# A normalizer sum moved from the tensor engine to the vector engine, and the normalizer used three MLP tiles later

## Chip, cores, metric

The kernel runs on one core of a Trainium2 chip. The metric is the device time of one execution in microseconds (us), lower is better. PE is the tensor engine, PEld its weight loads, DVE the vector engine, ACT the scalar engine, POOL the GpSimd engine, SP the engine that issues most DMAs (40 of 64 issues in the trace of the kernel before). A trace covers one execution from its first to its last recorded instruction (the span); the timed figure is some 2 us longer than the span.

## The reference, cut to what matters

```python
x = A_x                                        # [1, 2048, 512], bf16
phi = lambda t: where(t > 0, t + 1, exp(t)) + 1e-6
pq, pk = phi(q), phi(k)                        # 32 heads of 16
kv  = einsum("bhsd,bhse->bhde", pk, v)
z   = einsum("bhsd->bhd", pk)                  # <- the sum in question: over all 2048 tokens
num = einsum("bhqd,bhde->bhqe", pq, kv)
den = einsum("bhqd,bhd->bhq", pq, z)[..., None] + 1e-6
a   = merge_heads(num / den) @ wo
b   = token_mlp(layernorm(x))                  # w1: 2048 -> 1792, gelu, w2: 1792 -> 2048
g   = sigmoid((x * gate_w).sum(-1, keepdims=True))
out = g * a + (1 - g) * b
```

## The kernel before: the parts that matter

Tokens are cut into 16 tiles of 128. The order on PE is: *key steps* (kacc = x Wk for a tile, then gacc += x^T pk with a lag of four tiles), *query steps* (three uacc matmuls of the MLP and four qacc matmuls per step), *MLP tiles* (sixteen uacc matmuls each, numbered 3 to 13), and *output tiles* (four aps and fourteen yps matmuls each).

The sum z is taken over tokens. Tokens lie in 16 tiles x 128 partitions, so there are two sums: over the tiles and over the partitions. Before, both were matmuls. The first one takes the sixteen pk tiles through a 128x32 selector in four column tiles of the array (the sixteen take 1.24 us in the chain below; sixteen full ones would take 16 x 0.216 = 3.46):

```python
def z_tile(t):
    g = t % 4
    mm(zacc[32 * g : 32 * g + 32, :], zsel[:], pk[:, t, :], t < 4, t >= NT - 4,
       tile_position=(0, 32 * g))
...
for t in range(NT - LAG, NT):       # the last four key tiles
    g_tile(t)
    if t == NT - 3:                 # between gacc of tile 13 and of tile 14
        for u in range(NT):
            z_tile(u)
...                                 # DVE: zhi = bf16(zacc); zhl = odd * zhi - zacc
def kv_matmuls():                   # in query step 4
    ...
    zps = bank("zps")
    for j in range(ND):             # the sum over partitions: 4 matmuls of 8 columns
        mm(zps[:, 8 * j : 8 * j + 8], zhl[:, j * P : (j + 1) * P], neg8[:], True, True)
    ...                             # DVE: Z32 = zps * mask
...
for j in range(NB0, NF):            # MLP tiles 3..13
    ...                             # 16 uacc matmuls, gelu on ACT
    if j == NB0:
        den_matmuls()               # 16 column-tiled denps matmuls; DVE: rden = 1 / denps
        rden_chain()                # rden to DRAM, 16 broadcast loads rex, 16 pqT *= rex on DVE
    elif j <= NB0 + ND:
        w2_matmul(j - NB0 - 1)
```

The gate sums (sixteen DVE instructions, sum of x times gate_w) stood between the query steps and the reciprocal.

Of the kernel before, what the change touches and what calls it, by code (L numbers as in the profile page):

```python
# [8 lines left out]
ALU = mybir.AluOpType  # L9
AX = mybir.AxisListType  # L10
BF16 = mybir.dt.bfloat16
FP32 = mybir.dt.float32
# [3 lines left out]
def kernel(  # L16
# [13 lines left out]
    nc = tc.nc  # L30
    P = nc.NUM_PARTITIONS
    EPS = 1e-5
    PHI_EPS = 1e-6
    HEAD = 16
# [3 lines left out]
    S, D = X.shape  # L38
    F = B_w1.shape[1]
    NT = S // P  # L40
    ND = D // P
    NF = F // P
    SC = 512
    NSC = S // SC
# [14 lines left out]
    work = ctx.enter_context(tc.tile_pool(name="work", bufs=3))  # L59
    opool = ctx.enter_context(tc.tile_pool(name="opool", bufs=4))  # L60
    dpool = ctx.enter_context(tc.tile_pool(name="dpool", bufs=1, space=bass.MemoryType.DRAM))
    ps = ctx.enter_context(tc.tile_pool(name="ps", bufs=8, space=bass.MemoryType.PSUM))

    def keep(shape, dtype, name):
        return persist.tile(shape, dtype, name=name, tag=name)

    def bank(name, dtype=FP32):
        return ps.tile([P, SC], dtype, name=name, tag="bank")

    xs = keep([P, NT, D], BF16, "xs")  # L70
# [6 lines left out]
    pqT = keep([P, ND, S], BF16, "pqT")  # L77
    pk = keep([P, NT, D], BF16, "pk")
# [2 lines left out]
    W2sb = keep([P, ND, D], BF16, "W2sb")  # L81
    Z32 = keep([P, ND * 40], BF16, "Z32")
    zhi = keep([P, D], BF16, "zhi")
    zhl = keep([P, D], BF16, "zhl")
    odd = keep([P, 1], FP32, "odd")
    neg8 = keep([P, 8], BF16, "neg8")
    zsel = keep([P, 32], BF16, "zsel")
    rden = keep([P, SC], BF16, "rden")
    ident = keep([P, P], BF16, "ident")
    mask = keep([P, P], BF16, "mask")  # L90
    maskH = keep([P, 8], BF16, "maskH")
    gw_b = keep([P, D], BF16, "gw_b")
# [6 lines left out]
    gpre = keep([P, NT], FP32, "gpre")  # L99
# [8 lines left out]
    def mm(o, lhsT, rhs, start, stop, **kw):  # L108
        nc.tensor.matmul(o, lhsT=lhsT, rhs=rhs, start=start, stop=stop, **kw)  # L109
# [39 lines left out]
    for c, (j0, nb) in enumerate(w1_chunks):  # L149
        w = wpool.tile([P, NT, FB * P], BF16, name="w1c", tag="wc")  # L150
        w1c.append(w)
        for t0 in range(0, NT, 8) if c == 0 else (0,):
            t1 = t0 + 8 if c == 0 else NT
            nc.sync.dma_start(
                out=w[:, t0:t1, : nb * P], in_=w1_view[:, t0:t1, j0 * P : (j0 + nb) * P]
# [5 lines left out]
    nc.vector.memset(ones_f[:], 1.0)  # L161
    nc.vector.memset(mhalf[:], -0.5)
    nc.vector.memset(Z32[:], 0.0)
    nc.vector.memset(zsel[:], 0.0)
    nc.vector.memset(zsel[:, 0:2], 1.0)
    nc.vector.memset(neg8[:], -1.0)
    nc.gpsimd.memset(ident[:], 0.0)
    nc.gpsimd.affine_select(
        out=ident[:], in_=ident[:], compare_op=ALU.not_equal, fill=1.0, base=0,
        pattern=[[-1, P]], channel_multiplier=1,  # L170
    )
    nc.vector.tensor_reduce(out=odd[:], in_=ident[:, 1:P:32], op=ALU.add, axis=AX.X)
    block_mask(mask[:].rearrange("p (a b) -> p a b", b=HEAD), P // HEAD, HEAD)
    block_mask(maskH[:].rearrange("p (a b) -> p a b", b=1), 8, 1)

# [64 lines left out]
    def ln_shift(g):  # L240
        s = slice(g * TPC, (g + 1) * TPC)
        nc.vector.scalar_tensor_tensor(  # L242
            out=nmr[:, s], in0=mv[:, s, 0], scalar=-1.0, in1=rstd[:, s],
            op0=ALU.mult, op1=ALU.mult,
        )
# [22 lines left out]
            )  # L268
        phi(pqT[:, j, c * SC : (c + 1) * SC], qacc)

    def z_tile(t):
        g = t % 4
        mm(
            zacc[32 * g : 32 * g + 32, :], zsel[:], pk[:, t, :], t < 4, t >= NT - 4,
            tile_position=(0, 32 * g),
        )

    def ln_step(u):
        ln_stats(u)
        if u % TPC == TPC - 1:  # L280
            ln_rstd(u // TPC)
# [19 lines left out]
    for t in range(HEADS, NT):  # L301
# [8 lines left out]
            ln_apply(t - APPLY)  # L310
        if t % TPC == 0 and t >= 2 * TPC:
            ln_shift(t // TPC - 2)
    zacc = bank("zacc")
    for t in range(NT - LAG, NT):
        g_tile(t)
        if t == NT - 3:
            for u in range(NT):
                z_tile(u)
    ln_shift(2)
    ln_apply(NT - APPLY)  # L320
    nc.vector.tensor_copy(out=zhi[:], in_=zacc[:])
    nc.vector.scalar_tensor_tensor(
        out=zhl[:], in0=zhi[:], scalar=odd[:], in1=zacc[:], op0=ALU.mult, op1=ALU.subtract
    )

    gT = persist.tile([P, ND, D], BF16, name="gT", tag="wk_sb")
    for k in range(ND):
# [5 lines left out]
    def gelu(j, acc):  # L333
        nc.scalar.activation(  # L334
            out=uT[:, j, :], in_=acc[:], func=ACT.Gelu_apprx_tanh, bias=bcol[:, j : j + 1]
        )
# [6 lines left out]
    def kv_matmuls():  # L343
        kvps = bank("kvps")
        for j in range(ND):
            for k in range(ND):
                mm(
                    kvps[:, j * P : (j + 1) * P], wv_sb[:, k, j * P : (j + 1) * P],
                    gT[:, k, j * P : (j + 1) * P], k == 0, k == ND - 1,
                )  # L350
        nc.vector.tensor_tensor(
            out=kvbdT[:], in0=kvps[:].rearrange("p (j d) -> p j d", j=ND),
            in1=mask[:].unsqueeze(1).to_broadcast([P, ND, P]), op=ALU.mult,
        )
        zps = bank("zps")
        for j in range(ND):
            mm(zps[:, 8 * j : 8 * j + 8], zhl[:, j * P : (j + 1) * P], neg8[:], True, True)
        nc.vector.tensor_tensor(
            out=Z32[:].rearrange("p (j m) -> p j m", m=40)[:, :, 0:8],
            in0=zps[:, 0:32].rearrange("p (j m) -> p j m", m=8),  # L360
            in1=maskH[:].unsqueeze(1).to_broadcast([P, ND, 8]), op=ALU.mult,
        )

    def w2_matmul(j):
        wps2 = bank("wps2")
        mm(wps2[:], kvbdT[:, j, :], wo_sb[:, j, :], True, True)
        nc.scalar.activation(out=W2sb[:, j, :], in_=wps2[:], func=ACT.Copy)
# [12 lines left out]
    NB0 = 3  # L380
    accs = [bank("uacc") for _ in range(NB0)]
    for t in range(NT):
        for jj in range(NB0):
            mm(accs[jj][:], w1c[0][:, t, jj * P : (jj + 1) * P], hs[:, t, :], t == 0, t == NT - 1)
        q_block(t)
        if 2 <= t < 2 + LN_LAG:
            ln_step(NT - LN_LAG + t - 2)
        if t == 3 + LN_LAG:
            ln_shift(3)
        if 1 <= t < 5 or 7 <= t < 11:  # L390
            ln_apply(t + 7 if t < 5 else t + 5)
        if t == 1:
            biases()
        if t == 4:
            kv_matmuls()
    for jj in range(NB0):
        gelu(jj, accs[jj])

    for t in range(NT):
        junk = work.tile([P, D], BF16, name="junk", tag="junk", bufs=2)  # L400
        nc.vector.tensor_tensor_reduce(
            out=junk[:], in0=xs[:, t, :], in1=gw_b[:], scale=1.0, scalar=0.0,
            op0=ALU.mult, op1=ALU.add, accum_out=gpre[:, t : t + 1],
        )

    def rden_chain():
        rd_dram = dpool.tile([P, SC], BF16, name="rd_dram", tag="rd_dram")
        nc.gpsimd.dma_start(out=rd_dram[:], in_=rden[:])
        for c in range(NSC):
            for j in range(ND):  # L410
                rex = work.tile([P, SC], BF16, name="rex", tag="rex", bufs=4)
                src = rd_dram[32 * c + 8 * j : 32 * c + 8 * j + 8, :]
                nc.gpsimd.dma_start(out=rex[:], in_=src.unsqueeze(1).to_broadcast([8, HEAD, SC]))  # L413
                seg = pqT[:, j, c * SC : (c + 1) * SC]
                nc.vector.tensor_tensor(out=seg, in0=seg, in1=rex[:], op=ALU.mult)  # L415

    w2c = []

# [5 lines left out]
    for j in range(NB0, NF):  # L424
        c, jj = divmod(j, FB)
        acc = bank("uacc")
        for t in range(NT):
            mm(acc[:], w1c[c][:, t, jj * P : (jj + 1) * P], hs[:, t, :], t == 0, t == NT - 1)
        gelu(j, acc)
        if j == NB0:  # L430
            den_matmuls()
            rden_chain()
        elif j <= NB0 + ND:
            w2_matmul(j - NB0 - 1)
        if jj == FB - 1 or j == NF - 1:
            load_w2(c)

# [2 lines left out]
        out=gg[:], in0=gth[:], scalar1=0.5, scalar2=0.5, op0=ALU.mult, op1=ALU.add  # L440
    )
    nc.vector.tensor_scalar(
        out=c1[:], in0=gth[:], scalar1=-0.5, scalar2=0.5, op0=ALU.mult, op1=ALU.add
# [3 lines left out]
    for t in range(NT):  # L447
        c, tl = divmod(t, TPC)
        aps = bank("aps")
        for j in range(ND):  # L450
            mm(aps[:], pqT[:, j, t * P : (t + 1) * P], W2sb[:, j, :], j == 0, j == ND - 1)
        a_sc = work.tile([P, D], FP32, name="a_sc", tag="a_sc", bufs=2)
        nc.scalar.activation(  # L453
            out=a_sc[:], in_=aps[:], func=ACT.Identity,
            scale=gg[:, t : t + 1], bias=c2[:, t : t + 1],
        )
        parts = 2 if t == NT - 1 else 1
        W = D // parts
        for h in range(parts):
            cs = slice(h * W, (h + 1) * W)  # L460
            yps = bank("yps")
            for f in range(NF):
                mm(
                    yps[:, :W], w2c[c][:, f, tl * P : (tl + 1) * P], uT[:, f, cs],
                    f == 0, f == NF - 1,
                )
            ot = opool.tile([P, D], BF16, name="ot", tag="ot")
            nc.vector.scalar_tensor_tensor(  # L468
                out=ot[:, :W], in0=yps[:, :W], scalar=c1[:, t : t + 1], in1=a_sc[:, cs],
                op0=ALU.mult, op1=ALU.add,  # L470
            )
            nc.sync.dma_start(out=o_view[:, t, cs], in_=ot[:, :W])


# [28 lines left out]
```

## Time and profile before

| | before |
|---|---|
| time, median of 6 runs | 168.38 us (168.2 to 168.5) |
| span of the trace | 166.4 us |
| PE busy | 161.0 us, 97% |
| DVE busy | 79.8 us, 48% |
| granted PE clock | 1.000 |

The profile page of the kernel before gives for each engine the busy time in us, its share of the span and the instructions:

```profile
PE 161.0 (97%) x798; PEld 74.3 (45%) x798; DVE 79.8 (48%) x189; ACT 58.3 (35%) x90; POOL 18.2 (11%) x37
```

The chain that ended last, kernel before: start in us, length in us, what. The chain runs back from the last instruction, at each step to what released it or to the instruction before it on its engine; it is printed in order of time.

```profile
10.95 1.02 PE gacc L109 x4
...
30.17 2.59 PE gacc L109 x12
32.76 1.24 PE zacc L109 x16
34.00 1.83 PE gacc L109 x8
35.83 0.65 PE uacc L109 x3
...
43.44 0.89 PE kvps L109 x16
44.33 0.08 PE zps L109 x4
44.41 0.67 PE uacc L109 x3
...
64.51 0.98 PE denps L109 x16
65.48 3.56 PE uacc L109 x16
...
100.99 0.86 PE aps L109 x4
...
163.22 0.48 DVE ot L468
```

From 10.95 us on, the chain stays on PE until the last output is scaled. A full 128x512 matmul costs 0.216 us there (0.86 us for four). So the price of the tile sum can be read directly: 1.24 us of zacc, and 0.10 us more in the eight gacc behind it, which take 1.83 us where 8 x 0.216 is 1.73. The sixteen uacc behind the sixteen denps matmuls, 128x32 as well, are as much longer: 3.56 us where 16 x 0.216 is 3.46.

What DVE does at the end of the key steps and in two query steps, from the timeline of the kernel before (start, length, engine, line, operation, tiles, and in brackets what an idle time before it waited for):

```profile
32.56 0.29 DVE L209 TENSOR_SCALAR e<-e 128x512 bf16<-128x512 bf16 x1
32.88 0.69 DVE L212 SCALAR_TENSOR_TENSOR pk<-kacc,e 128x512 bf16<-128x512 f32 x1
...
60.21 0.29 DVE L209 TENSOR_SCALAR e<-e 128x512 bf16<-128x512 bf16 x1 [0.49 <-ACT e L208]
60.54 0.69 DVE L212 SCALAR_TENSOR_TENSOR pqT<-qacc,e 128x512 bf16<-128x512 f32 x1
61.72 0.29 DVE L209 TENSOR_SCALAR e<-e 128x512 bf16<-128x512 bf16 x1 [0.49 <-ACT e L208]
```

A query step is 1.51 us long (60.21 to 61.72) and DVE waits 0.49 us in each. And pk of the last key tile ends at 33.57 us, in the middle of the zacc matmuls, which need it.

### The profile page before, as it was taken

What the parts mean: (1) busy time and instruction counts of PE and PEld (TensorE: products, weight loads), DVE (VectorE), ACT (ScalarE), POOL (GpSimd) and SP (SyncE); (2) the same over time, 40 slices, a digit from 0 to 9 for tenths busy, and PEclk for the clock granted to TensorE, in tenths of its full rate; (3) what the DMA queues carried; (4) which work ended last, traced back from release to release, by engine and by line L of the source; (5) the groups of instructions that cost most, each with busy time, mean ns of one, the idle gap of its engine ahead of it and who ended that gap; (6) DMA issues with size and microseconds to landing.
All of it is one profiled execution on the core that took longest, in us unless ns stands there. A gap on an engine that the chain in (4) does not pass through costs nothing.

```text
span 166.4 us, 2087 instructions
## 1 busy us (share of the span) xinstructions
PE 161.0 (97%) x798; PEld 74.3 (45%) x798; DVE 79.8 (48%) x189; ACT 58.3 (35%) x90; POOL 18.2 (11%) x37
## 2 busy tenths in 40 slices
PE   7799999999999999999999999999999999999992
PEld 3434444434544444444444444444444444444461
DVE  1569999986986769992302412151222111111121
ACT  3263374927658557222222111051111222211110
POOL 5000512110020000002712521000000000000000
PEclk9999999999999999999999999999999999999999
DMA  5999999999900002900598499941100000110001
GB/s 157 229 256 255 348 354 310 349 349 345 242 1 2 0 0 65 357 23 32 185 294 196 138 322 262 309 159 63 35 32 32 32 33 32 46 52 32 32 32 32
DMA packets 29993, 25.05 MB, mean 151 GB/s; under 512 B 7776, under 2 KB 29408, under 8 KB 29984
## 3 DMA queue, kind: packets, MB, share of 16 engines
q1 hardware_dynamic: 27968, 22.02, 44.3%
q0 software_dynamic: 1440, 2.38, 5.6%
q10 hardware_dynamic: 576, 0.52, 1.1%
q8 instruction: 6, 0.10, 0.3%
q14 instruction: 3, 0.02, 0.0%
HBM read 21.11 MB, written 2.23 MB: 140 GB/s over the span
## 4 chain that ended last, share of the span: by engine, by line
PE 93%; DMA 3%; DVE 1%; SPq 1%; ACT 0%; issue 0%
PE uacc L109 29%; PE yps L109 29%; PE gacc L109 8%; PE qacc L109 8%; PE aps L109 8%; PE kacc L109 8%; DMA wk_sb<-in_A_wqkv_dram 3%; PE zacc L109 1%; PE denps L109 1%; PE kvps L109 1%; PE wps L109 1%; SPq L125 1%; DVE pk L212 0%; ACT e L208 0%; DVE ot L468 0%
## 5 line engine op out<-in xcount | busy, mean ns | idle before, releaser
L109 PE MATMUL uacc<-hs,w1c 128*128 128x512 bf16 x224 | 51.9, 379 | 0.0
L109 PE MATMUL yps<-uT,w2c 128*128 128x512 bf16 (+1 forms) x238 | 51.0, 367 | 0.0
L109 PEld LDWEIGHTS <-w2c 128*128 128x128 bf16 x238 | 23.3, 98 | 25.3
L109 PEld LDWEIGHTS <-w1c 128*128 128x128 bf16 x224 | 21.7, 98 | 26.2 <-issue 0.4
L468 DVE SCALAR_TENSOR_TENSOR ot<-yps,c,a_sc 128x512 bf16<-128x512 f32 (+1 forms) x17 | 12.1, 719 | 42.3 <-PE yps L109 41.4
L453 ACT ACTIVATE a_sc<-aps,c,gg 128x512 f32<-128x512 f32 x16 | 12.3, 777 | 46.8 <-PE aps L109 39.1
L415 DVE TENSOR_TENSOR pqT<-pqT,rex 128x512 bf16<-128x512 bf16 x16 | 6.5, 424 | 26.5 <-DMA rex<-rd_dram 26.5
L334 ACT ACTIVATE uT<-uacc,bcol 128x512 bf16<-128x512 f32 x14 | 9.3, 687 | 27.5 <-PE uacc L109 27.5
L109 PE MATMUL kacc<-wk_sb,xT 128*128 128x512 bf16 x64 | 15.8, 379 | 1.0 <-DMA wk_sb<-in_A_wqkv_dram 1.0
L109 PE MATMUL qacc<-xT,wq_sb 128*128 128x512 bf16 x64 | 16.4, 379 | 0.0
L109 PE MATMUL aps<-W2sb,pqT 128*128 128x512 bf16 x64 | 16.4, 379 | 0.0
L109 PE MATMUL gacc<-pk,xs 128*128 128x512 bf16 x64 | 15.9, 379 | 0.2 <-DVE pk L212 0.2
L248 ACT ACTIVATE hs<-xs,nmr,rstd 128x512 bf16<-128x512 bf16 x16 | 12.8, 805 | 3.1 <-DVE nmr L242 3.1
L209 DVE TENSOR_SCALAR e<-e 128x512 bf16<-128x512 bf16 x32 | 9.1, 284 | 9.1 <-ACT e L208 9.1
L208 ACT ACTIVATE e<-qacc 128x512 bf16<-128x512 f32 x16 | 9.6, 597 | 10.2 <-PE qacc L109 9.3
L208 ACT ACTIVATE e<-kacc 128x512 bf16<-128x512 f32 x16 | 9.0, 596 | 9.5 <-PE kacc L109 9.5
L212 DVE SCALAR_TENSOR_TENSOR pqT<-qacc,e 128x512 bf16<-128x512 f32 x16 | 11.1, 692 | 0.5
L212 DVE SCALAR_TENSOR_TENSOR pk<-kacc,e 128x512 bf16<-128x512 f32 x16 | 11.1, 692 | 0.6
L413 POOL DMA_DIRECT2D rex<-rd_dram x16 | 9.4, 593 | 15.9 <-DVE pqT L415 13.1
L232 DVE BATCH_NORM_STATS2 stats<-xs 128x6 f32<-128x512 bf16 x16 | 10.9, 683 | 0.0
L109 PEld LDWEIGHTS <-xT 128*128 128x128 bf16 x64 | 6.3, 98 | 8.6 <-ACT xT L202 1.2
L109 PEld LDWEIGHTS <-xs 128*128 128x128 bf16 x64 | 6.2, 98 | 8.4 <-issue 1.2
(66 smaller groups left out, 68.2 us busy)
## 6 DMA issues: line engine op xcount, KB each, us to landing
w2c<-in_B_w_dram SPq DMA_DIRECT2D x4, 1792.0 KB, 10.2
w1c<-in_B_w_dram SPq DMA_DIRECT2D x2, 2048.0 KB, 16.3
w1c<-in_B_w_dram SPq DMA_DIRECT2D x3, 1024.0 KB, 11.6
rex<-rd_dram POOLq DMA_DIRECT2D x16, 128.0 KB, 6.7
out_dram<-ot SPq DMA_DIRECT2D x15, 128.0 KB, 1.7
xs<-in_A_x_dram SPq DMA_DIRECT2D x3, 512.0 KB, 4.2
wq_sb<-in_A_wqkv_dram SPq DMA_DIRECT2D x1, 512.0 KB, 4.9
wv_sb<-in_A_wqkv_dram SPq DMA_DIRECT2D x1, 512.0 KB, 11.8
```

The lines of the kernel that those rows point to most:

```text
L109: nc.tensor.matmul(o, lhsT=lhsT, rhs=rhs, start=start, stop=stop, **kw)
L125: q.dma_start(out=xs[:, t0 : t0 + n, :], in_=x_view[:, t0 : t0 + n, :])
L208: nc.scalar.activation(out=e[:], in_=acc[:], func=ACT.Exp)
L209: nc.vector.tensor_scalar(out=e[:], in0=e[:], scalar1=1.0, scalar2=PHI_EPS, op0=ALU.min, op1=ALU.add)
L212: nc.vector.scalar_tensor_tensor(out=dst, in0=acc[:], scalar=0.0, in1=e[:], op0=ALU.max, op1=ALU.add)
L232: nc.vector.bn_stats(out=stats[:], in_=xs[:, t, :])
L248: nc.scalar.activation(out=hs[:, t, :], in_=xs[:, t, :], func=ACT.Identity, scale=rstd[:, t : t + 1], bias=nmr[:, t : t + 1],)
L334: nc.scalar.activation(out=uT[:, j, :], in_=acc[:], func=ACT.Gelu_apprx_tanh, bias=bcol[:, j : j + 1])
L413: nc.gpsimd.dma_start(out=rex[:], in_=src.unsqueeze(1).to_broadcast([8, HEAD, SC]))
L415: nc.vector.tensor_tensor(out=seg, in0=seg, in1=rex[:], op=ALU.mult)
L453: nc.scalar.activation(out=a_sc[:], in_=aps[:], func=ACT.Identity, scale=gg[:, t : t + 1], bias=c2[:, t : t + 1],)
L468: nc.vector.scalar_tensor_tensor(out=ot[:, :W], in0=yps[:, :W], scalar=c1[:, t : t + 1], in1=a_sc[:, cs], op0=ALU.mult, op1=ALU.add,)
```

## The change

The intent: take the sum over tiles off PE, which is on the chain, and give it to DVE, which has idle time in the query steps. Fifteen fp32 adds make zacc: ten in query steps 6 to 15 and five behind them. Then zacc is split into two bf16 halves, and the sum over partitions takes eight small matmuls instead of four. Because zacc is complete later, the normalizer (denps) and what hangs on it move three MLP tiles back, the gate sums behind the reciprocal, and the last two of four chunks of the multiplication by rden into the output loop.

```diff
-    def z_tile(t):            # 16 column-tiled matmuls, removed
+    def z_add(t):
+        first = pk[:, 0, :] if t == 1 else zacc[:]
+        nc.vector.tensor_tensor(out=zacc[:], in0=first, in1=pk[:, t, :], op=ALU.add)
...
     for t in range(NT - LAG, NT):
         g_tile(t)
-        if t == NT - 3:
-            for u in range(NT):
-                z_tile(u)
...
+    def z_split():
+        nc.vector.tensor_copy(out=zhi[:], in_=zacc[:])
+        nc.vector.tensor_tensor(out=zlo[:], in0=zacc[:], in1=zhi[:], op=ALU.subtract)
+
+    def z_matmuls():
         zps = bank("zps")
         for j in range(ND):
-            mm(zps[:, 8 * j : 8 * j + 8], zhl[:, j * P : (j + 1) * P], neg8[:], True, True)
+            for i, part in enumerate((zhi, zlo)):
+                mm(zps[:, 8 * j : 8 * j + 8], part[:, j * P : (j + 1) * P], ones8[:],
+                   i == 0, i == 1)
...
         if t == 4:
             kv_matmuls()
+        if t >= 6:
+            z_add(t - 5)
...
+    for t in range(11, NT):
+        z_add(t)
+    z_split()
...
-        if j == NB0:
+        if j == NB0 + 2:
+            z_matmuls()
+        if j == NB0 + 3:
             den_matmuls()
-            rden_chain()
-        elif j <= NB0 + ND:
-            w2_matmul(j - NB0 - 1)
+            gate_sums()                      # stood before the MLP tiles
+            rden_chunk(0)
+            rden_chunk(1)                    # chunks 2 and 3: behind output tiles 1 and 2
+        if NB0 + 4 <= j < NB0 + 4 + ND:
+            w2_matmul(j - NB0 - 4)
```

More of the change, by code (lines that the diff above doesn't have):

```diff
@@ L83 @@
     zhi = keep([P, D], BF16, "zhi")
-    zhl = keep([P, D], BF16, "zhl")
-    odd = keep([P, 1], FP32, "odd")
-    neg8 = keep([P, 8], BF16, "neg8")
-    zsel = keep([P, 32], BF16, "zsel")
+    zlo = keep([P, D], BF16, "zlo")
+    zacc = keep([P, D], FP32, "zacc")
+    ones8 = nc.const_aps.tensor(1.0, (P, 8), BF16)
     rden = keep([P, SC], BF16, "rden")
@@ L163 @@
     nc.vector.memset(Z32[:], 0.0)
-    nc.vector.memset(zsel[:], 0.0)
-    nc.vector.memset(zsel[:, 0:2], 1.0)
-    nc.vector.memset(neg8[:], -1.0)
     nc.gpsimd.memset(ident[:], 0.0)
@@ L171 @@
     )
-    nc.vector.tensor_reduce(out=odd[:], in_=ident[:, 1:P:32], op=ALU.add, axis=AX.X)
     block_mask(mask[:].rearrange("p (a b) -> p a b", b=HEAD), P // HEAD, HEAD)
@@ L269, in q_block @@
         phi(pqT[:, j, c * SC : (c + 1) * SC], qacc)
-    def z_tile(t):
-        g = t % 4
-        mm(
-            zacc[32 * g : 32 * g + 32, :], zsel[:], pk[:, t, :], t < 4, t >= NT - 4,
-            tile_position=(0, 32 * g),
-        )
+    def z_add(t):
+        first = pk[:, 0, :] if t == 1 else zacc[:]
+        nc.vector.tensor_tensor(out=zacc[:], in0=first, in1=pk[:, t, :], op=ALU.add)
     def ln_step(u):
@@ L312 @@
             ln_shift(t // TPC - 2)
-    zacc = bank("zacc")
     for t in range(NT - LAG, NT):
         g_tile(t)
-        if t == NT - 3:
-            for u in range(NT):
-                z_tile(u)
     ln_shift(2)
     ln_apply(NT - APPLY)
-    nc.vector.tensor_copy(out=zhi[:], in_=zacc[:])
-    nc.vector.scalar_tensor_tensor(
-        out=zhl[:], in0=zhi[:], scalar=odd[:], in1=zacc[:], op0=ALU.mult, op1=ALU.subtract
-    )
     gT = persist.tile([P, ND, D], BF16, name="gT", tag="wk_sb")
@@ L354, in kv_matmuls @@
         )
+    def z_split():
+        nc.vector.tensor_copy(out=zhi[:], in_=zacc[:])
+        nc.vector.tensor_tensor(out=zlo[:], in0=zacc[:], in1=zhi[:], op=ALU.subtract)
+    def z_matmuls():
         zps = bank("zps")
         for j in range(ND):
-            mm(zps[:, 8 * j : 8 * j + 8], zhl[:, j * P : (j + 1) * P], neg8[:], True, True)
+            for i, part in enumerate((zhi, zlo)):
+                mm(
+                    zps[:, 8 * j : 8 * j + 8], part[:, j * P : (j + 1) * P], ones8[:],
+                    i == 0, i == 1,
+                )
         nc.vector.tensor_tensor(
@@ L395, with gate_sums, rden_chunk @@
             kv_matmuls()
+        if t >= 6:
+            z_add(t - 5)
     for jj in range(NB0):
         gelu(jj, accs[jj])
-    for t in range(NT):
-        junk = work.tile([P, D], BF16, name="junk", tag="junk", bufs=2)
-        nc.vector.tensor_tensor_reduce(
-            out=junk[:], in0=xs[:, t, :], in1=gw_b[:], scale=1.0, scalar=0.0,
-            op0=ALU.mult, op1=ALU.add, accum_out=gpre[:, t : t + 1],
-        )
-    def rden_chain():
-        rd_dram = dpool.tile([P, SC], BF16, name="rd_dram", tag="rd_dram")
-        nc.gpsimd.dma_start(out=rd_dram[:], in_=rden[:])
-        for c in range(NSC):
-            for j in range(ND):
-                rex = work.tile([P, SC], BF16, name="rex", tag="rex", bufs=4)
-                src = rd_dram[32 * c + 8 * j : 32 * c + 8 * j + 8, :]
-                nc.gpsimd.dma_start(out=rex[:], in_=src.unsqueeze(1).to_broadcast([8, HEAD, SC]))
-                seg = pqT[:, j, c * SC : (c + 1) * SC]
-                nc.vector.tensor_tensor(out=seg, in0=seg, in1=rex[:], op=ALU.mult)
+    for t in range(11, NT):
+        z_add(t)
+    z_split()
+    def gate_sums():
+        for t in range(NT):
+            junk = work.tile([P, D], BF16, name="junk", tag="junk", bufs=2)
+            nc.vector.tensor_tensor_reduce(
+                out=junk[:], in0=xs[:, t, :], in1=gw_b[:], scale=1.0, scalar=0.0,
+                op0=ALU.mult, op1=ALU.add, accum_out=gpre[:, t : t + 1],
+            )
+    rd_dram = dpool.tile([P, SC], BF16, name="rd_dram", tag="rd_dram")
+    def rden_chunk(c):
+        if c == 0:
+            nc.gpsimd.dma_start(out=rd_dram[:], in_=rden[:])
+        for j in range(ND):
+            rex = work.tile([P, SC], BF16, name="rex", tag="rex", bufs=4)
+            src = rd_dram[32 * c + 8 * j : 32 * c + 8 * j + 8, :]
+            nc.gpsimd.dma_start(out=rex[:], in_=src.unsqueeze(1).to_broadcast([8, HEAD, SC]))
+            seg = pqT[:, j, c * SC : (c + 1) * SC]
+            nc.vector.tensor_tensor(out=seg, in0=seg, in1=rex[:], op=ALU.mult)
     w2c = []
@@ L472 @@
             nc.sync.dma_start(out=o_view[:, t, cs], in_=ot[:, :W])
+        if 0 < t < NSC - 1:
+            rden_chunk(t + 1)
 _INS = ['A_x', 'A_wqkv', 'A_wo', 'B_x', 'B_w1', 'B_b1', 'B_w2', 'B_b2', 'gate_w']
```

## The prediction, made before the changed kernel was run

> What bounds the kernel now. The page's busy line gives PE 161.0 us of a 166.4 us span (97%), DVE 48%, ACT 35%; the granted clock is 1.000. The chain that ended last is 93% PE, and from 10.95 us to 163.22 us it is unbroken PE work. In that stretch a 128x512 matmul costs 0.216 us (four gacc: 0.86 us; fourteen yps: 3.02 us). So only what leaves or enters PE's order counts, unless another engine becomes late.
>
> What the change removes. In the chain the sixteen zacc matmuls take 1.24 us (32.76 to 34.00), and the eight gacc after them 1.83 us where 8 x 0.216 is 1.73: the way back from 128x32 column tiles costs about 0.10 us more. The timeline shows why 1.24 and not about 0.98, as for the sixteen denps matmuls: the last zacc needs pk of tile 15, whose DVE instruction ends at 33.57. [...] Removed from PE: 1.34 us, all on the chain. Without zacc, gacc of tile 15 reaches PE at about 33.62, just when its pk is ready, so the wait for pk comes back by at most 0.1 us.
>
> What it adds to PE. zps has eight matmuls of 8 columns instead of four. The four cost about 0.10 us (kvps, zps and the three uacc after them take 1.64 us; 16 x 0.0556 + 0.65 is 1.54). Eight, between long matmuls and each with its own weight load, I estimate at 0.2 to 0.45 us. Net add about 0.25 us. The denps matmuls move three MLP tiles later at unchanged cost (0.98 + 0.11 us).
>
> What it moves to DVE. Fifteen adds of 128x512, fp32 output. [...] Query steps last 1.51 us; DVE does 0.33 + 0.60 us in each and would do about 1.53 us with an add. It keeps up, within 0.5 us after ten steps. Five chained adds (3.6 us) and the split (about 1.3 us) end near 67 us, PE reaches zps near 70 us: no wait. Released PSUM banks have over 2 us of slack.
>
> Later: reciprocal (3.35 us) ends near 78 us, gate sums (16 x 0.61 us) near 88, multiplications of chunk 0 near 90 to 92, before PE needs them at about 99.7. Chunk 1 near 100, needed at 115. The gate vectors c1 and c2 come earlier than before (109 us). Chunk 3 may hold up one ot by 1 to 3 us; four output tiles of PSUM cover it.
>
> Predicted: 168.4 - 1.34 + 0.25 = 167.3 us. Range 166.9 to 167.9. Chances: faster by over 2%: 0.02; within 2%: 0.95; slower by over 2%: 0.03.
>
> What would show it. Chain: no zacc; query steps begin about 1.3 us earlier and still last 1.51 us; zps 0.2 to 0.45 us; no new PE wait. Groups: add x15, near 0.69 us each. Waits: none of PE on zlo, Z32 or pqT. DVE's busy share rises to about 53%.
>
> What would make it wrong. Adds of 1 us or more would make the query steps DVE-bound through the PSUM banks and delay the split past zps. rex loads slowed by the w2 loads beyond 99 us would stop PE at the first aps. A small zps weight load that isn't hidden at all would cost up to 0.8 us and eat most of the gain.

The 0.10 us that the eight gacc take longer is read from the chain. The trace of the kernel before has no 128x512 fp32 add. It has other DVE instructions of 128x512 with records of 683 to 692 ns. After one of them the next that does not need its result starts 0.60 us later (pk at 32.88, stats at 33.48 us), one that needs it 0.72 us later (zhi at 34.35, zhl at 35.07). The 0.60 and 0.72 us in the prediction are these; that an fp32 add would be like them was the estimate. The "over 2 us of slack" of the PSUM banks is an estimate too; the test is e5, where the last pqT starts some 7 us later than in e7 (67.47 against 60.53) and PE's query steps keep their length.

## The result

| | before | after |
|---|---|---|
| time, median | 168.38 us (6 runs, 168.2 to 168.5) | 167.23 us (6 runs, 166.71 to 167.47) |
| ratio of fast runs | | 0.993, 95% interval 0.9915 to 0.9945 |
| span of the trace | 166.4 us | 165.1 us |
| first gacc to end of the last ot, in the chain | 152.75 us | 151.67 us |
| DVE busy | 48% | 53% |

A ratio here is the mean time of one kernel's fast runs over that of the other's fast runs of the same rounds, so not quite the ratio of the medians. The fourth row is the steadiest measure: it leaves out the start, which differs from trace to trace (first gacc between 10.68 and 11.03 us in the thirteen traces), and of 1.3 us between the two spans 0.27 us are that start (first gacc at 10.95 and 10.68 us). The change did not cause these 0.27 us: the same changed kernel starts at 10.91 us in e0. The row is worked out from the chain: 163.22 + 0.48 - 10.95 before, 161.87 + 0.48 - 10.68 after.

The busy line of the page, kernel after:

```profile
PE 160.4 (97%) x786; PEld 74.5 (45%) x786; DVE 87.6 (53%) x200; ACT 58.5 (35%) x90; POOL 18.3 (11%) x37
```

The chain that ended last, kernel after:

```profile
10.68 1.02 PE gacc L108 x4
...
29.90 3.45 PE gacc L108 x16
...
33.36 1.02 PE gacc L108 x4
34.38 0.65 PE uacc L108 x3
...
69.86 0.18 PE zps L108 x8
70.04 3.47 PE uacc L108 x16
73.52 0.98 PE denps L108 x16
74.49 3.56 PE uacc L108 x16
...
99.64 0.86 PE aps L108 x4
...
161.87 0.48 DVE ot L473
```

There is no zacc on PE, and the chain is still nothing but PE from the first gacc to the last ot. The last four gacc take 1.02 us instead of 0.86: the wait for pk of tile 15 that zacc used to absorb. Eight zps cost 0.18 us and 0.02 more in the uacc tile behind them.

DVE in the last query step and behind it, from the timeline of the kernel after:

```profile
58.87 0.29 DVE L204 TENSOR_SCALAR e<-e 128x512 bf16<-128x512 bf16 x1
59.19 0.69 DVE L207 SCALAR_TENSOR_TENSOR pqT<-qacc,e 128x512 bf16<-128x512 f32 x1
59.80 0.68 DVE L268 TENSOR_TENSOR zacc<-zacc,pk 128x512 f32<-128x512 f32 x1
60.40 0.29 DVE L204 TENSOR_SCALAR e<-e 128x512 bf16<-128x512 bf16 x1
60.72 0.69 DVE L207 SCALAR_TENSOR_TENSOR pqT<-qacc,e 128x512 bf16<-128x512 f32 x1
61.33 4.32 DVE L268 TENSOR_TENSOR zacc<-zacc,pk 128x512 f32<-128x512 f32 x6
65.68 0.43 DVE L341 CAST zhi<-zacc 128x512 bf16<-128x512 f32 x1
66.14 0.69 DVE L342 TENSOR_TENSOR zlo<-zacc,zhi 128x512 bf16<-128x512 f32 x1
70.08 0.19 DVE L352 TENSOR_TENSOR Z<-zps,maskH 128x32 bf16<-128x32 f32 x1 [3.25 <-PE zps L108]
```

The add fills DVE's idle time: its step is now 1.53 us (58.87 to 60.40), PE's 1.51. An add takes 0.68 us by its record, but the next instruction that does not need it starts 0.60 us after it; in the chained run at the end it is 0.72 us. zlo is ready at 66.83 us, PE comes to zps at 69.86, DVE waits 3.25 us for PE and not the other way round.

### The profile page after: what moved, and what is told of

Same layout as the page of the kernel before. It is cut to its first block, busy times and chain, and to the rows that moved or that the text cites. A ratio compares the mean times of both kernels' runs of the same rounds, so it can differ in the third digit from the quotient of the medians.

```text
span 165.1 us, 2073 instructions
## 1 busy us (share of the span) xinstructions
PE 160.4 (97%) x786; PEld 74.5 (45%) x786; DVE 87.6 (53%) x200; ACT 58.5 (35%) x90; POOL 18.3 (11%) x37
## 4 chain that ended last, share of the span: by engine, by line
PE 93%; DMA 3%; DVE 1%; SPq 0%; ACT 0%; issue 0%
PE uacc L108 29%; PE yps L108 29%; PE gacc L108 9%; PE qacc L108 8%; PE aps L108 8%; PE kacc L108 8%; DMA wk_sb<-in_A_wqkv_dram 3%; PE denps L108 1%; PE kvps L108 1%; PE wps L108 1%; SPq L124 0%; DVE pk L207 0%; ACT e L203 0%; DVE ot L473 0%; DVE e L204 0%
## 5 line engine op out<-in xcount | busy, mean ns | idle before, releaser
L401 DVE CUSTOM_DVE_ANT_0 junk<-xs,gw_b 128x512 bf16<-128x512 bf16 x16 | 9.8, 684 | 0.0
```

The lines of the kernel that those rows point to most:

```text
L401: nc.vector.tensor_tensor_reduce(out=junk[:], in0=xs[:, t, :], in1=gw_b[:], scale=1.0, scalar=0.0, op0=ALU.mult, op1=ALU.add, accum_out=gp ...
```

## Experiments

Theory: PE's order is all that counts; the gain is the zacc matmuls and the 0.10 us more in the gacc behind them, less what comes back on PE. The adds are free because they fit into DVE's idle time, and the move has the one purpose to give DVE time to finish. Rivals: the gain comes from the later normalizer (a calmer time for its DMAs and for DVE); or the adds cost something that hides part of a larger gain. Unless it is said otherwise, the result of a kernel was correct. e4 to e7 ran on another chip than the rest, so kernels of different calls are best compared by the ratio column; one run of the kernel before in that call and one in the last call were slow (170.50 and 170.34 us, both at a clock of 0.996) and are left out of the ratios.

All kernels at a glance. The chain column is first gacc to end of the last ot; "surplus" is against the changed kernel's own 151.66 us.

| kernel | time, median us | ratio to before (95%) | chain us | surplus us |
|---|---|---|---|---|
| e0 changed kernel, again | 167.07 | 0.9939 (0.9927 to 0.9951) | 151.66 | 0 |
| e1 move alone | 168.29 | 1.0008 (0.9995 to 1.0021) | 152.74 | 1.08 |
| e2 zacc matmuls gone, nothing else | 167.12 | 0.9939 (0.9927 to 0.9952) | 151.55 | -0.11 |
| e3 phi of tile 15 first | 167.06 | 0.9939 (0.9927 to 0.9951) | 151.50 | -0.16 |
| e4 normalizer one tile earlier | 167.79 | 0.9976 (0.9959 to 0.9993) | 152.30 | 0.64 |
| e5 twice the adds' work | 178.06 | 1.0573 (1.0547 to 1.0598) | 162.29 | 10.63 |
| e6 adds in the key steps | 175.66 | 1.0416 (1.0357 to 1.0475) | 160.50 | 8.84 |
| e7 all adds behind | 172.03 | 1.0227 (1.0211 to 1.0243) | 156.55 | 4.89 |
| e8 the same, PE kept busy | 170.77 | 1.0149 (1.0125 to 1.0172) | 155.15 | 3.49 |
| e9 as e3 | 167.15 | 0.9933 (0.9914 to 0.9952) | 151.50 | -0.16 |
| e10 changed kernel, third time | 167.06 | 0.9929 (0.9907 to 0.9950) | 151.66 | 0 |

### The changed kernel again (e0)

No edit. It ran on one chip with the next three.

> The changed kernel itself, beside the next three on one chip. All theories: 167.2 us, about 1.1 to 1.2 us under the kernel before. In the chain the stretch from the first gacc to the first uacc is 23.7 us (24.9 before), and from the first uacc to the first aps 65.3 us (65.2 before).

Measured: 167.07 us; first gacc to first uacc 23.68 us (10.91 to 34.59), first uacc to first aps 65.26 us. As expected.

### The move alone (e1)

```diff
 # the kernel before, zacc matmuls and zps as they were
-        if j == NB0:
+        if j == NB0 + 3:
             den_matmuls()
-            rden_chain()
+            gate_sums()
+            rden_chunk(0)
+            rden_chunk(1)
 # chunks 2 and 3 behind output tiles 1 and 2, w2_matmul three tiles later
```

> The kernel before with the sixteen zacc matmuls kept on PE and only the move made: denps, gate sums and the rden loads three MLP tiles later, the last two chunks in the output loop. Theory (only PE's order counts): no gain, 168.4 us plus or minus 0.15. Rival (the gain comes from the later normalizer and its calmer DMA and DVE): 167.2 to 167.6 us. In the chain zacc stays at about 1.24 us.

The chain of e1 still has zacc:

```profile
32.83 1.23 PE zacc L109 x16
```

Measured: 168.29 us, ratio 1.0008. The move is worth nothing by itself. The first rival falls.

### The zacc matmuls gone, nothing else (e2, wrong result)

```diff
-    zacc = bank("zacc")
+    zacc = keep([P, SC], FP32, "zacc")
+    nc.vector.memset(zacc[:], 16.0)
 ...
-        if t == NT - 3:
-            for u in range(NT):
-                z_tile(u)
```

> The kernel before without the zacc matmuls: zacc is an SBUF constant, so the result is wrong on purpose; nothing is moved and no add is made. Theory: the whole gain, 1.18 us less than before (1.34 us of matmuls and switch gone, 0.16 us of wait for pk of tile 15 come back): 167.2 us, and within 0.1 us of the changed kernel, from which it differs on PE only by four zps matmuls (0.10 us). Rival: 167.8 us or more, if the move has a part in the gain; or 167.0 or less, if the DVE adds cost the changed kernel something.

The chain of e2 at the end of the key steps:

```profile
30.16 4.47 PE gacc L109 x20
```

Measured: 167.12 us, the ratio of the changed kernel to the fourth digit. In the chain it is 0.11 us shorter than the changed kernel, which is what the four zps more cost. So removing the matmuls makes the whole gain, and the fifteen adds cost nothing that shows: the second rival falls too. How the gain divides into matmuls (1.24 us) and longer gacc behind them (0.10 us) is read from the chain before; no run removes one without the other.

### The wait for pk of tile 15 (e3, e9, and e10 beside it)

```diff
-        if t > LAG:
+        if t == NT - 1:
+            ln_step(NT - 2 - LN_LAG)      # statistics of tile 11, behind phi of tile 15
+        if t > LAG and t != NT - 2:
             ln_step(t - LN_LAG)
```

> The changed kernel with DVE's phi of key tile 15 ahead of the LayerNorm statistics of tile 11. Theory: pk of tile 15 is then ready about 1 us earlier, the 0.16 us before the last four gacc (1.02 us in the chain, 0.86 without a wait) vanish, and the time is 0.16 us below the changed kernel, 167.05 us; the first uacc starts 23.54 us after the first gacc. Rival (the 1.02 us is something else at the end of the key steps, such as a weight load): it stays, and the time too.

The chain of e3:

```profile
30.00 4.32 PE gacc L108 x20
34.32 0.65 PE uacc L108 x3
```

The twenty gacc take 4.32 us = 20 x 0.216, where the changed kernel had 3.45 + 1.02 = 4.47. So the reading of the wait was right: it was DVE's order, and the chain is 0.16 us shorter. The time did not follow: 167.06 against 167.07 us. Both kernels were run again to decide it.

> The kernel with the phi of key tile 15 first, once more. In the first try the chain lost the wait as expected (twenty gacc 4.32 us instead of 4.47) but the times did not differ: 167.06 against 167.07 us. Theory: 0.15 us of the chain is 0.15 us of the time, hidden by the spread of the runs: 0.1 to 0.2 us below the changed kernel beside it. Rival: the gain is given back elsewhere, no difference again.

> The changed kernel once more, for the comparison with the kernel that does the phi of key tile 15 first: 167.1 us, twenty gacc 4.47 us.

Measured: 167.15 us for the edited kernel, 167.06 for the changed one. Over eleven runs each, the means are 167.12 and 167.09 us. All four traces agree about the chain (151.50 us with the edit, 151.66 without), and the timed runs do not show it: the difference of the means is +0.03 us, uncertain by some 0.12 us (an estimate from the spread of the runs), so -0.16 does not fit. In these four traces it is not given back outside the part that is compared: the first gacc starts at 10.83 us on average with the edit and at 10.82 without, and 2.72 us of span follow the end of the last ot in both. Where the 0.16 us go in the timed runs was not found. It stays open. No faster version than the changed kernel came out of this.

### The normalizer one tile earlier (e4)

```diff
-        if j == NB0 + 2:
+        if j == NB0 + 1:
             z_matmuls()
-        if j == NB0 + 3:
+        if j == NB0 + 2:
             den_matmuls()
 ...    # gate sums, rden chunks 0 and 1 and w2_matmul move one tile earlier with it
```

> The changed kernel with the normalizer one MLP tile earlier (zps behind MLP tile 4, denps behind 5). Theory: zlo is ready at 66.8 us of the changed kernel's trace, PE reaches zps at 66.4: a wait of 0.4 to 0.5 us, 167.65 us. Rival (DVE's adds have more slack than that reading says): no wait, 167.2 us.

The chain of e4 around zps:

```profile
66.16 0.70 DVE zlo L342
...
66.90 0.33 PE zps L108 x7
67.23 3.47 PE uacc L108 x16
```

The wait list of this trace puts 0.5 us of waiting of zps on zlo, and from there the chain goes back through DVE. zps itself takes 0.33 us on the chain instead of 0.18. Together 0.64 us in the chain, 167.79 us in time. The slack reading (3 us at the third tile, none at the second) holds. Behind the third MLP tile is the earliest place between two tiles for zps without a wait, and one tile less already costs more than half of the gain.

### Twice the work of the adds (e5)

```diff
         nc.vector.tensor_tensor(out=zacc[:], in0=first, in1=pk[:, t, :], op=ALU.add)
+        nc.vector.tensor_tensor(out=zacc[:], in0=zacc[:], in1=zacc[:], op=ALU.max)
```

> The changed kernel with a second, idle DVE instruction (maximum of zacc with itself, result unchanged) behind each of the fifteen adds. Theory: a query step of DVE takes about 0.33 + 0.60 + 0.72 + 0.60 = 2.25 us against PE's 1.51; the lag grows by 0.74 us a step, the PSUM banks still cover it, and the last twelve chained instructions and the split end near 77.6 us, when PE has reached zps at 69.9: a wait of 7 to 8 us, about 175 us. Rival 1 (DVE still has room): 167.2. Rival 2 (the banks run out): the query steps of PE themselves get longer than 1.51 us.

The chain of e5 around zps:

```profile
77.25 0.70 DVE zlo L343
...
78.00 0.35 PE zps L108 x7
78.35 6.00 PE uacc L108 x16
```

The split ended at 77.95 us where 77.6 was expected, and the query steps on PE kept their length (25.10 us of work in the 25.10 us from 34.60 to 59.70). So neither rival holds: DVE is full (9.95 of 10.30 us busy from 59.70 to 70 us), and the banks do cover its lag. But the time is 3 us above the expected 175. The trace says where: the uacc tile behind the wait takes 6.00 us instead of 3.47. That is a new term, tested in e7 and e8.

### The adds in the key steps (e6)

```diff
         g_tile(t - LAG)
+        z_add(t - LAG + 1)             # twelve in the key steps, three behind them
 ...
-        if t >= 6:
-            z_add(t - 5)               # and none in or behind the query steps
```

> The changed kernel with twelve of the fifteen adds in the key steps instead of the query steps, three behind them. DVE works without a break there in the changed kernel (18.4 of 19.2 us) and pk of tile 15 comes 0.16 us late already. Theory: 12 x 0.60 = 7.2 us more DVE work is about 7 us more for PE: 174 us. Rival (the four tiles of lag between pk and gacc cover some of it): 168 to 171 us.

Measured: 175.66 us, 8.6 more than the changed kernel beside the theory's 7. Adds that are free in the query steps stop PE here, because DVE had hardly any idle time in the key steps (18.4 of 19.2 us busy in the changed kernel, from 10.7 to 29.9 us). In the chain the last four gacc start at 40.01 us instead of 33.36, 6.7 us later (6.6 counted from the first gacc), near the 7.2 us of work added. That gacc group and the uacc and qacc groups behind it take 4.77 us in the chain instead of 2.53, 2.24 us more, and that is the rest of the 8.84. It goes with a lower clock, as in e5, in stretches of e6 (columns: stretch, its length, busy time and count of PE, PEld, DVE, ACT, POOL, granted clock, DMA share, GB/s):

```profile
34.00:36.00 2.00, 0.86 (x4) 0.38 (x4) 1.97 (x6) 1.81 (x3) 0.00 (x0) 1.00 1.10 349
36.00:38.00 2.00, 0.70 (x3) 0.19 (x2) 1.93 (x6) 2.00 (x4) 0.00 (x0) 0.93 1.09 347
38.00:40.00 2.00, 1.10 (x3) 0.30 (x2) 1.90 (x7) 0.08 (x1) 0.89 (x1) 0.50 1.10 349
```

No single wait of PE here was longer than 1.4 us by the wait list; PE was busy for 0.86 and 0.70 us of two stretches of 2 us, and the clock fell to 0.50. It stayed there to 44 us and was 0.72 in the stretch from 44 to 45 and 1.00 behind it.

The four timed runs of e6 agree: three had a mean clock of 0.98 to 0.99 and took 175.4 to 175.9 us, and the one at 1.000 took 173.67 us, 6.6 above the changed kernel and close to the 174 that the theory expected.

### All adds behind the query steps (e7), and the same with PE kept busy (e8)

```diff
 # e7
-        if t >= 6:
-            z_add(t - 5)
 ...
-    for t in range(11, NT):
+    for t in range(1, NT):
         z_add(t)
 # e8, besides
         if j == NB0 + 2:
+            fill = bank("fill")
+            for _ in range(15):
+                mm(fill[:], hs[:, 0, 0:P], hs[:, 1, :], True, True)
             z_matmuls()
```

> The changed kernel with all fifteen adds behind the query steps, none in them. Theory: they start near 61.3 us, chained at 0.72 us they end near 72.1 and the split at 73.3; PE reaches zps at 69.9 and waits 3.4 us: 170.6 us. Rival (the adds in the query steps cost PE something, so that taking them out gives some back): query steps under 1.51 us.

Measured: 172.03 us, 1.4 above the 170.6 expected. The split ends at 73.18 us as expected, the query steps did not get shorter, so the adds in them cost PE nothing. The granted clock in e7 (columns as above), and the uacc tile behind zps in its chain:

```profile
core 0: us, PE busy (x) PEld busy (x) DVE busy (x) ACT busy (x) POOL busy (x), PEclk, DMA share, GB/s
70.00:73.20 3.20, 0.18 (x1) 0.10 (x1) 3.04 (x5) 0.62 (x1) 0.00 (x0) 0.94 0.00 0
73.20:78.50 5.30, 5.27 (x27) 2.13 (x31) 0.19 (x1) 0.04 (x1) 0.00 (x0) 0.71 0.01 3
78.50:100.00 21.50, 21.50 (x112) 9.63 (x105) 16.15 (x41) 6.04 (x10) 7.74 (x13) 1.00 0.50 158
...
73.58 4.84 PE uacc L108 x16
```

PE is idle for some 3.3 us, and in the 5.3 us behind it runs at 0.71 of its clock; the uacc tile there takes 4.84 us instead of 3.47. The sum is wait 3.3 + zps 0.17 + clock 1.37 = 4.84 us, against 4.89 us in the chain. In stretches of 1 us the clock is 0.91 from 72 to 73 us and 0.50 from 73 to 74, so it fell some 3 us after PE's last full matmul; it is 0.88 from 76 to 77 and 1.00 from 77, so it came back after some 3 us of work. In e5 the clock fell after 3 us too (0.56 from 73 to 74 us), but after the wait it stayed at 0.50 for about 5.4 us of work, to about 83.4 us (an estimate from the 0.50 of the stretches up to 82 us and the 0.66 of 82 to 84). That the idle time is what lowers the clock is so far only a reading of these stretches. To test it, e8 fills the wait with matmuls of no use.

> The kernel with all adds behind the query steps took 172.0 us, 1.4 us more than its wait of 3.4 us explains, and its trace shows a granted clock of 0.71 in the 5.3 us after the wait. This one is the same, with fifteen 128x512 matmuls of no use (15 x 0.216 = 3.2 us, into a PSUM bank that nothing reads) between the last uacc before zps and zps, so that PE works through the wait. Theory (the surplus is the clock, taken back because PE stood idle): granted clock 1.000 throughout, the uacc tile after zps 3.5 us instead of 4.8, total 170.6 us. Rival (the surplus is a later wait, of DVE or DMA work that came late): it stays near 172 us.

The same stretch and the same tile in e8:

```profile
70.00:73.20 3.20, 3.20 (x16) 1.47 (x15) 3.03 (x6) 0.69 (x1) 0.00 (x0) 1.00 0.00 1
73.20:78.50 5.30, 5.21 (x44) 2.14 (x42) 0.60 (x3) 0.69 (x1) 0.00 (x0) 1.00 0.01 3
...
73.85 3.47 PE uacc L108 x16
```

Measured: 170.77 us, the uacc tile behind zps 3.47 us. The wait is the same, DVE's work is the same; only the clock is back, and with it 1.3 us. So a wait of PE in this kernel can have two prices: its own length and the slow restart. e7 paid both (wait 3.3 us, restart 1.37); e4, with a wait of 0.5 us, had 3.47 us for the uacc tile behind it and no restart to pay. e5 has the same sum: PE is ready for zps at about 70.1 us in its own trace (first uacc at 34.59, and 35.48 us from there as in the changed kernel), so the wait is 7.9 us, and zps 0.17 and the clock 6.00 - 3.47 = 2.53 more make 10.6.

## Why the prediction was right, point by point

It said 167.3 us (166.9 to 167.9) and 167.23 was measured; the reading that only PE's order counts was tested by e1 and e2 and holds. The terms, from the two chains:

| term on PE | predicted us | measured us | from |
|---|---|---|---|
| zacc matmuls gone | -1.24 | -1.24 | chain before |
| extra length of the eight gacc behind zacc, gone | -0.10 | -0.10 | 1.83 - 8 x 0.216 |
| wait for pk of tile 15 comes back | at most +0.10, not in the sum | +0.16 | 1.02 - 0.86 |
| zps, eight instead of four | +0.25 | +0.10 | 0.18 + 0.02, less about 0.10 before |
| sum | -1.09 | -1.08 | chain 152.75 to 151.67 |

Two terms were mis-sized: zps by 0.15 us, and the returning wait, left out of the sum, by 0.16 us the other way. That the sum agrees to 0.01 us is luck; that the two large terms and the path were right is not:

- zps: "Eight, between long matmuls and each with its own weight load, I estimate at 0.2 to 0.45 us" and "Net add about 0.25 us". The 0.20 us measured is at the lower edge, and the net is 0.10. The eight start 25 ns after each other; the timeline of the kernel after has them at 69.70, 69.73, 69.75 and so on. That makes 8 x 25 ns = 0.2 us. The trace before already gave it: four cost about 0.10 us there, so eight 0.20.
- The returning wait: "the wait for pk comes back by at most 0.1 us" was 0.16 us. e3 shows that DVE's order causes it.

Right as stated: the adds ("near 0.69 us each", 0.68 by their records, 0.60 and 0.72 us apart); the query steps of 1.53 us on DVE against 1.51; a split that ends "near 67 us" (66.83) and zps "near 70" (69.86); chunk 0 multiplied between 88 and 90 us; no wait of PE on zlo, Z32 or pqT; DVE 53% busy. The gate vectors were ready at 100.96 us instead of 109.

Wrong in details that did not reach the chain: "Chunk 1 near 100" was 93.9 us, and "Chunk 3 may hold up one ot by 1 to 3 us" did not happen. The rex loads took 2.9 us at the median instead of the 6.7 of the trace before; the prediction does not say which it reckoned with.

Of the prediction's own list of what could go wrong, the first item was tested. e5 made DVE's step longer than PE's: the split came late by 11 us, but the banks did not run out, so "DVE-bound through the PSUM banks" was not the way it failed. The other two items were not tested; they only did not occur. The rex loads were in time (chunk 1 was multiplied at 93.9 us, PE came to the first aps at 99.64), and the weight loads of zps were mostly hidden: eight records of 0.096 us each, 0.77 us together, which is the "up to 0.8 us", in 0.20 us of the chain. And no step of the prediction had the clock in it: had PE waited as long as in e7 (3.3 us), the loss would have been underestimated, in e7 by 1.37 us.

## What to carry to other kernels

When the chain is one engine without a gap, cost a change by that engine's instructions alone, with start-to-start distances from the chain and not with record lengths (here 0.216 us against 0.379 for a full matmul, 25 ns against 166 for a zps); then check stage by stage that the engine which takes over the work has idle time in that very stage, because adds that were free in one stage cost 8.6 us, 2.2 of them through the clock, when twelve of them stood in the stage before. A later use of the result is worth nothing in itself; it buys slack, and one tile too little cost more than half of the gain. If an experiment makes the tensor engine wait, look at the granted clock before looking for a second cause: here it fell to 0.50 in a wait of 3.3 us (e7), which cost 1.37 us more, and in e6 it fell to 0.50 with a row of waits of at most 1.4 us.
